# A fused attention, expert and gated-MLP kernel: its first pair of heads loaded, measured and transposed in another order

## The chip, the cores and the metric

The kernel runs on one NeuronCore of a Trainium2 chip. Its engines are TensorE (PE: matmuls and transposes, with PEld its weight loads), VectorE (DVE), ScalarE (ACT), GpSimd (POOL) and the sequencer SyncE (SP), and 16 DMA engines move data. Each engine works through its own instructions in the order in which they were written, and semaphores tie the engines together. The metric is the device time of one execution in microseconds, as the median of several runs.

## The reference

Three layers follow each other for 8 batches of 576 rows. The first is block-causal attention over 8 heads of 64, the second a mixture of four causal attention experts of which the best two are added, the third a gated MLP with a spatial mix over the rows.

```python
def _attn_ref(q, k, v):                       # 8 x 8 x 576 x 64
    scores = scale * np.matmul(q, k.transpose(0, 1, 3, 2))
    mask = block_i >= block_j                 # blocks of 64
    scores = np.where(mask, scores, -1000000000.0)
    scores = scores - np.max(scores, axis=-1, keepdims=True)
    attn = np.exp(scores)
    attn = attn / (np.sum(attn, axis=-1, keepdims=True) + 1e-09)
    return np.matmul(attn, v).astype(np.float32)

def _moe_ref(x, w_gate, wq, wk, wv, wo):      # 4 experts, 2 of them used
    logits = x @ w_gate
    for e in range(E):
        q = x @ wq[e]; k = x @ wk[e]; v = x @ wv[e]
        scores = np.where(causal, -1000000000.0, scale * (q @ k.transpose(0, 2, 1)))
        a = np.exp(scores - scores.max(-1, keepdims=True))
        a /= a.sum(-1, keepdims=True) + 1e-09
        out += (gate weight of e) * (a @ v @ wo[e])

def _moe2_ref(x, w_in, w_spatial, b_spatial, w_out):
    h = np.maximum(x @ w_in, 0.0)
    u, v = (h[..., :d_ff // 2], h[..., d_ff // 2:])
    v_n = (v - mu) / np.sqrt(var + 1e-06)
    v_s = np.einsum('ts,bsd->btd', w_spatial, v_n) + b_spatial[None, :, None]
    return ((u * v_s) @ w_out).astype(np.float32)
```

## The kernel before

Every float32 operand is scaled by a power of two and split into two float16 halves, a high and a low one, and each product is three float16 matmuls (high by high, high by low, low by high; `PROD`). The scale of an operand comes from its own size, so nothing can be split before its size is known. The work goes by batch, and in a batch by pairs of heads: four pairs of the attention, two pairs of the experts, and then the gated MLP.

A pair begins with loads. `load_qk` issues seven DMAs (line 257: both heads of q and both of k, 128 KB each; line 261: the last 64 rows of q, head by head; line 263: the last 64 rows of k) into a tile `nat`, and `load_v` three more (lines 271 and 274). `mags` then takes the size of the operand in each partition, on VectorE as a largest magnitude (line 297, written to `mst`) or on ScalarE as a sum of magnitudes (line 295, with its accumulator). In batches 1 to 7 one scale serves all four pairs. In batch 0 each pair has a scale of its own for q and k, so that the first pair doesn't wait for the others: `scale0` turns the two columns of sizes by a transpose on TensorE (line 200), takes their maxima (203), spreads them on a diagonal (206), and `scale2` sends that to all partitions by a matmul with ones (211) and makes powers of two of it on VectorE (218 to 227: `ne`, `sc`, `in`; 324 and 326: `es`). `prep_qk` transposes q and k on TensorE (line 345) and splits them: ScalarE writes the high half (233), VectorE the low one (239), both into `qk`. Then come the scores in four parts j = 0 to 3 (393, with a mask 403; 408 for j = 3), their row maxima on VectorE (414, 416), a bias (424 on ScalarE or 426 on VectorE), the exponentials on ScalarE (430, 435), the split of the weights (352 to 356, 451, 455), DMA transposes (460), the product with v (470), and the split of its result (499, 504), which another DMA transpose (506) brings into `x` for the dense part.

The constants and zeroed paddings at the kernel's head are memsets and selects on VectorE and GpSimd (lines 97 to 192, with line 371 further down); the memset in line 284 is the last of VectorE's before the first `mags`. The weights are loaded and split once, between the first pairs (`startup`). At the end of each batch the gated MLP normalises `vf` in five chunks of rows: line 921 shifts and scales, 924 casts on ScalarE, 929 subtracts, each chunk on VectorE or GpSimd as a letter in a table says.

The order is written out by hand in two tables. Some 1,370 steps (`add` lists them, with what each needs) are cut at every `yield` into pieces, `ORDER` names the step of each next piece, 3,671 entries in all, and `WAYS` names the engine for steps that could run on more than one ("D" VectorE, "A" ScalarE, "G" GpSimd, "S" SyncE for loads). In `WAYS`, the entry `lq.0` holds the queue of the first pair's `load_qk` for each batch, `mg.0.0` the engine of its first `mags`. The costs that `add` carries (`pe`, `act`, `dve`, `loads`) are the numbers with which the tables were planned; they don't enter the program. Loads on the SP and ACT queues take their semaphores in turn out of eight, so that the ninth load waits for the first to land.

In batch 0 a step `pq` (that is, `prep_qk`) needs the step `s2o` (`scale2` of the pair) before its first piece, the transposes, since its scale is used in the second.

Of the kernel before, what the change touches and what calls it, by code (L numbers as in the profile page):

```python
# [10 lines left out]
F32 = mybir.dt.float32  # L11
# [12 lines left out]
P = 128  # L24
# [12 lines left out]
def attn_moe_gmlp_kernel(  # L37
# [211 lines left out]
    def load_qk(b, pr, way):  # L249
        dma = dict(S=nc.sync, A=A, G=G)[way].dma_start  # L250
# [26 lines left out]
    def mags(b, pr, i, way):  # L277
# [8 lines left out]
        a = slice(0, 2) if i == 0 else slice(2, 3)  # L286
        st = s.st
        o = slice(pr, pr + 1)
        if b == 0 and i == 0:
            s.own[pr] = Obj()  # L290
            s.own[pr].st = st = cst.tile([P, 2, 1], F32, name=f"mst{pr}")
            o = slice(0, 1)
# [40 lines left out]
    def prep_qk(b, pr, i):  # L333

        p, s = PD[b, pr], BS[b]
        if b == 0:
            s = s.own[pr]
        if i == 0:
            new_qk(p)
            p.es, p.nes = s.es[:, 0:1], s.es[:, 1:2]  # L340
        ps = duo()
        n = 640 if i == 0 else 576
        for c in range(NC):
            r = P if c < 4 or i == 0 else 64
            T.transpose(ps[:, P * c:P * c + r], p.nat[0:r, i, c, :], ident[0:r, 0:r])
        yield
        o = (p.q, p.k)[i]
        yield from split16(o[:, 0], o[:, 1], ps[:, 0:n], s.sc[:, i:i + 1], "A")
# [416 lines left out]
    def dense(b, keep):  # L765
# [831 lines left out]
```

## Time and profile before

| | us |
|---|---|
| median of 3 runs | 933.75 |
| lowest and highest | 932.49 to 935.44 |
| the profiled execution | 931.44 |
| its span, from the first to the last instruction | 929.7 |
| PE busy | 838.6 (90%) |
| DVE busy | 754.4 (81%) |
| ACT busy | 632.9 (68%) |
| POOL busy | 547.5 (59%) |
| DMA engines, mean rate | 155 GB/s |

The rows come from one profiled execution, with times in microseconds from the start of its span. The shares of busy time are averages over stages that differ: the stretch before the first matmul, a stretch in which the first batches and the weights are prepared, a long one in which the batches follow each other, and the last batch's tail. "PEclk" is the clock that TensorE was granted as a share of its full 2.4 GHz; 0.50 is the lower level, 1.2 GHz.

### The profile page before, as it was taken

To read this page: it belongs to the slowest core of one execution; us is meant where nothing else is said; L and a number is where in the kernel's file an instruction comes from. 1 tells how busy PE (TensorE), PEld (TensorE's weight loads), DVE (VectorE), ACT (ScalarE), POOL (GpSimd) and SP (SyncE) were. 2 spreads that over 40 slices of the span, in tenths; PEclk is the share of its full clock that TensorE was granted. 3 is DMA by queue.
4 is the path that set the end of the run, shared out by engine and by line. 5 is a ranking of instruction groups with operands and counts; after the bars stand their busy time and mean duration, and the time that the engine had idled before them with its cause. 6 is when DMAs were issued, how large, how long until landed. Compare 5 with 4: busy or idle time off the path is not lost. (4 is left out here: it accounts for less than half of the span.)

```text
span 929.7 us, 25206 instructions
## 1 busy us (share of the span) xinstructions
PE 838.6 (90%) x10038; PEld 616.4 (66%) x10038; DVE 754.4 (81%) x1608; ACT 632.9 (68%) x1151; POOL 547.5 (59%) x542
## 2 busy tenths in 40 slices
PE   3677887789998999989999999989999999999987
PEld 2466765567766767666776677567767786667554
DVE  6999989988998688887988799788997879468351
ACT  3867687866778777785776697675698568448232
POOL 6557457756677767785675867345857665425120
PEclk9777999599999999999999999999999999999999
DMA  9999889998789798999799799879699939914601
GB/s 202 217 220 191 185 178 177 193 158 133 164 152 201 112 186 149 197 189 169 137 159 197 133 149 199 145 138 181 139 180 171 158 58 155 202 30 77 140 1 57
DMA packets 470716, 143.66 MB, mean 155 GB/s; under 512 B 456003, under 2 KB 462499, under 8 KB 470598
## 3 DMA queue, kind: packets, MB, share of 16 engines
q1 hardware_dynamic: 461750, 129.72, 78.4%
q0 software_dynamic: 5232, 11.44, 4.9%
q8 instruction: 79, 1.29, 0.5%
q10 hardware_dynamic: 3616, 0.89, 0.5%
q14 instruction: 39, 0.32, 0.1%
HBM read 38.19 MB, written 9.44 MB: 51 GB/s over the span
## 5 line engine op out<-in xcount | busy, mean ns | idle before, releaser
L455 POOL TENSOR_TENSOR p<-pf,p 128x512 f16<-128x512 f32 (+1 forms) x198 | 242.5, 1247 | 74.7 <-DVE p L354 24.8
L414 DVE TENSOR_REDUCE st<-duo 128x2 f32<-128x1024 f32 (+2 forms) x192 | 151.2, 814 | 17.5 <-PE duo L401 8.8
L470 PEld LDWEIGHTS <-pT 128*128 128x128 f16 x4320 | 144.6, 99 | 28.2 <-DMA pT<-p 12.9
L435 ACT ACTIVATE pf<-duo,st,es 128x512 f32<-128x512 f32 (+3 forms) x224 | 122.4, 617 | 17.0 <-DVE st L426 14.2
L393 PE MATMUL duo<-qk 64*128 64x256 f16 (+3 forms) x1152 | 110.9, 315 | 20.6 <-DVE qk L239 7.7
L356 POOL TENSOR_SCALAR p<-pf 128x1024 f16<-128x1024 f32 (+1 forms) x68 | 78.0, 1149 | 86.5 <-ACT pf L435 55.9
L980 PE MATMUL duo<-wsp,vn 128*128 128x288 f16 x832 | 111.9, 286 | 2.1 <-ACT pf L435 1.1
L470 PE MATMUL duo<-v,pT 128*128 128x65 f16 (+1 forms) x2880 | 102.3, 196 | 10.2 <-DMA pT<-p 5.4
L804 PE MATMUL duo<-x,wqk 128*128 128x288 f16 x768 | 98.7, 286 | 2.1 <-DVE pf L499 0.7
L980 PEld LDWEIGHTS <-vn 128*128 128x128 f16 x832 | 80.0, 98 | 24.0 <-DVE vn L929 1.6
L804 PEld LDWEIGHTS <-wqk 128*128 128x128 f16 x768 | 74.3, 98 | 21.9 <-issue 2.9
L998 PE MATMUL duo<-wo,gT 128*128 128x512 f16 x384 | 86.0, 379 | 0.2 <-POOL gT L987 0.2
L393 PEld LDWEIGHTS <-qk 64*128 64x128 f16 x1152 | 46.2, 98 | 52.5 <-issue 33.0
L921 POOL TENSOR_SCALAR vf<-vf,nw 128x512 f32<-128x512 f32 (+1 forms) x27 | 25.8, 963 | 82.7 <-DVE nw L912 36.6
L435 ACT ACTIVATE pf<-duo,st,mt 128x256 f32<-128x256 f32 (+3 forms) x128 | 69.8, 617 | 5.3 <-DVE st L426 4.0
L451 DVE TENSOR_TENSOR p<-pf,p 128x1024 f16<-128x1024 f32 (+1 forms) x45 | 64.6, 1436 | 6.1 <-ACT p L352 5.8
L998 PEld LDWEIGHTS <-gT 128*128 128x128 f16 x384 | 36.6, 98 | 43.3 <-DVE gT L987 1.0
L504 POOL TENSOR_TENSOR xh<-pf,xh 128x640 f16<-128x640 f32 x30 | 44.8, 1494 | 32.9 <-ACT xh L352 26.6
L827 PE MATMUL duo<-wvg,x 128*128 128x260 f16 x480 | 56.5, 274 | 0.6 <-DVE nw L912 0.6
L352 ACT CAST p<-pf 128x1024 f16<-128x1024 f32 (+1 forms) x53 | 56.7, 1072 | 0.5
L470 PE MATMUL duo<-V,pT 128*128 128x65 f16 (+1 forms) x1440 | 49.6, 194 | 7.8 <-DMA pT<-p 5.2
L883 PE MATMUL duo<-wf,x 128*128 128x512 f16 x240 | 54.5, 379 | 1.8 <-DMA x<-xh 1.2
(273 smaller groups left out, 1732.2 us busy)
## 6 DMA issues: line engine op xcount, KB each, us to landing
out_dram<-pf SPq DMA_DIRECT2D x16, 512.0 KB, 3.3
nat<-in_q_dram SPq DMA_DIRECT2D x40, 128.0 KB, 3.2
nat<-in_k_dram SPq DMA_DIRECT2D x40, 128.0 KB, 3.2
wf<-in_moe_w_in_dram SPq DMA_DIRECT2D x8, 512.0 KB, 5.3
nat<-in_v_dram SPq DMA_DIRECT2D x32, 128.0 KB, 3.0
nat<-in_v_dram POOLq DMA_DIRECT2D x30, 128.0 KB, 4.6
nat<-in_q_dram POOLq DMA_DIRECT2D x22, 128.0 KB, 4.4
nat<-in_k_dram POOLq DMA_DIRECT2D x22, 128.0 KB, 4.4
```

The lines of the kernel that those rows point to most:

```text
L352: A.copy(hi, src)
L356: G.tensor_scalar(hi, src, 1.0, 1.0, op0=OP.mult, op1=OP.mult)
L393: T.matmul(ph[:, hh, o:o + w], p.q[hs, a, ts], p.k[hs, bb, 0:w], start=i == 0, stop=False)
L414: V.reduce_max(st[:, 0, 2 * c:2 * c + 2], ph[:, :, off[c]:off[c] + P * (c + 1)], axis=AX.X)
L435: A.activation(pf[:, n * hh + off[c]:n * hh + off[c] + w], ph[:, hh, off[c]:off[c] + w], AF.Exp, bias=st[:, 1, 2 * c + hh:2 * c + hh + 1], ...
L451: V.tensor_sub(lo, src, hi)
L455: G.tensor_sub(lo[:, z:z + m], src[:, z:z + m], hi[:, z:z + m])
L470: T.matmul(ps[:, hh, o:o + n], pT[:, col(t, kk):col(t, kk) + P], p.v[:, hh, kk, a:a + n], start=kk == 0 and i == 0, stop=kk == nk - 1 and ...
L804: T.matmul(ps[:, MID + a:MID + a + w], wqk16[:, l, c, 2 * n + i, :], x16[c][:, r, a:a + w], start=m == 0, stop=m == 11)
L827: T.matmul(ps[:, i, :260], x16[d][:, l, P * c:P * c + P], wvg16[:, r, d, :], start=m == 0, stop=m == 11)
L980: T.matmul(ps[:, MID + a:MID + a + n], l, wsp16[:, r, c, a:a + n], start=i == 0, stop=i == 13)
L998: T.matmul(ps[:, i], gT[:, x, d, P * c:P * c + P], wo16[:, y, d, :], start=m == 0, stop=m == 11)
```

## The change

The seven loads of the first pair of batch 0 are issued ahead of all others and go in turn to the SP and the ACT queue (way "M"). Its sizes are taken by two engines: `mags` has three steps for this pair, q on VectorE, k on ScalarE, and v (as before) later. In batch 0 the transposes of `prep_qk` need only the loads, and the scale only from the second piece on. `ORDER` and `WAYS` are written anew for the whole kernel; most entries stand within a few places of where they stood, and 50 steps, most of them in batches 1 to 7, run on another engine than before.

```diff
     def load_qk(b, pr, way):
-        dma = dict(S=nc.sync, A=A, G=G)[way].dma_start
+        each = iter((nc.sync, A) * 4) if way == "M" else None
+
+        def dma(*a):
+            (next(each) if each else dict(S=nc.sync, A=A, G=G)[way]).dma_start(*a)
...
         a = slice(0, 2) if i == 0 else slice(2, 3)
+        if b == 0 and pr == 0:
+            a = (slice(0, 1), slice(2, 3), slice(1, 2))[i]
         st = s.st
         o = slice(pr, pr + 1)
-        if b == 0 and i == 0:
-            s.own[pr] = Obj()
-            s.own[pr].st = st = cst.tile([P, 2, 1], F32, name=f"mst{pr}")
+        if b == 0 and i != 1:
+            if pr not in s.own:
+                s.own[pr] = Obj()
+                s.own[pr].st = cst.tile([P, 2, 1], F32, name=f"mst{pr}")
+            st = s.own[pr].st
             o = slice(0, 1)
...
         if i == 0:
             new_qk(p)
-            p.es, p.nes = s.es[:, 0:1], s.es[:, 1:2]
         ps = duo()
...
         yield
+        p.es, p.nes = s.es[:, 0:1], s.es[:, 1:2]
         o = (p.q, p.k)[i]
...
-        50, 54, 54, 50, 51, 50, 50, 50, 54, 50, 50, 52, 142, 142, 142, 143, 143, 51, 54, 54, 143, 143, 143, 143, 54,
+        50, 50, 50, 50, 50, 50, 50, 55, 55, 51, 55, 54, 52, 67, 143, 68, 143, 143, 144, 144, 51, 55, 144, 144, 144,
...
-        "last": ("A", "G", "G", "G", "G", "G", "A", "D"), "lq.0": ("A", "S", "S", "S", "G", "S", "S", "G"),
+        "last": ("D", "G", "G", "G", "G", "G", "A", "D"), "lq.0": ("M", "S", "S", "S", "S", "S", "S", "G"),
...
-            for i in range(2):
+            one = key == (0, 0)
+            for i in range(2 + one):
...
-                    [("PE", 0.73), act(n, each=0.15), dve(n, rate=1.06)], [("s2", b) if b else ("s2o", key)], [("pq", key, 0)] * i,
-                    ["duo"] + [("qk", key)] * (i == 0), ["duo"])
+                    [("PE", 0.73), act(n, each=0.15), dve(n, rate=1.06)], [("s2", b) if b else ("lq", key)], [("pq", key, 0)] * i,
+                    ["duo"] + [("qk", key)] * (i == 0), ["duo"], {} if b else {1: [("s2o", key)]})
```

Lines from 250 on move: what was line 345 is 351 after the change, 297 is 304, and from 346 on every line stands 7 lower.

On TensorE, at the program's head, the rows before are these (`nat` is the loaded pair, `mst` the sizes, `dgo` the diagonal with the maxima, `qk` the split operands):

```order
L1592 UNCONDITIONAL_BRANCH
L200 MATMUL duo<-ident,mst_198 2x128
L211 MATMUL duo<-dgo,ones 128x2
L345 MATMUL duo<-ident,nat 128x128 x9
L345 MATMUL duo<-ident,nat 128x64
L200 MATMUL duo<-ident,mst_234 2x128
L393 LDWEIGHTS qk
```

And these after the change:

```order
L1603 UNCONDITIONAL_BRANCH
L351 MATMUL duo<-ident,nat 128x128 x5
L200 MATMUL duo<-ident,mst_198 2x128
L351 MATMUL duo<-ident,nat 128x128 x4
L351 MATMUL duo<-ident,nat 128x64
L211 MATMUL duo<-dgo,ones 128x2
L200 MATMUL duo<-ident,mst_236 2x128
```

The ten transposes of the first pair stood behind the two small matmuls of its scale; now the five of q stand ahead of both, and the five of k between them.

On ScalarE's queue, at the program's head, before (L257, L261 and L263 are `load_qk`, L271 and L274 `load_v`):

```order
L175 ACTIVATE junk<-ones 128x1
L257 DMA nat<-in_q_dram 128x4x64 x2
L271 DMA nat<-in_v_dram 128x4x64
L257 DMA nat<-in_k_dram 128x4x64 x2
L261 DMA nat<-in_q_dram 64x64 x2
L263 DMA nat<-in_k_dram 64x2x64
L271 DMA nat<-in_v_dram 128x4x64
L274 DMA nat<-in_v_dram 64x2x64
L233 ACTIVATE qk<-duo,sco_206 128x640
L233 ACTIVATE qk<-duo,sco_206 128x576
```

After (L253 is now every load of `load_qk`, L302 the sizes on ScalarE):

```order
L175 ACTIVATE junk<-ones 128x1
L253 DMA nat<-in_q_dram 128x4x64
L253 DMA nat<-in_k_dram 128x4x64
L253 DMA nat<-in_q_dram 64x64
L274 DMA nat<-in_v_dram 128x4x64
L302 ACTIVATE junk,mst_198<-nat 128x640
L274 DMA nat<-in_v_dram 128x4x64
L277 DMA nat<-in_v_dram 64x2x64
L233 ACTIVATE qk<-duo,sco_217 128x640
```

Three of the pair's seven loads stay on this queue instead of all seven, the first load of v goes behind them, and the sizes of k stand between two loads of v. The other four go to SyncE's queue, ahead of the second pair's loads, which had stood first there.

On VectorE in the last batch's normalisation, the rows between the last small operation on `nw` and the scale of h (`neh`) were these before:

```order
L912 TENSOR_SCALAR nw<-mv 128x5
L921 TENSOR_SCALAR vf<-vf,nw 128x512 x2
L921 TENSOR_SCALAR vf<-vf,nw 64x512
L929 TENSOR_TENSOR vn<-vf,vn 128x512 x3
L929 TENSOR_TENSOR vn<-vf,vn 64x512
```

And these after:

```order
L919 TENSOR_SCALAR nw<-mv 128x5
L928 TENSOR_SCALAR vf<-vf,nw 128x512 x3
L936 TENSOR_TENSOR vn<-vf,vn 128x512
L928 TENSOR_SCALAR vf<-vf,nw 64x512
L936 TENSOR_TENSOR vn<-vf,vn 128x512 x2
L936 TENSOR_TENSOR vn<-vf,vn 64x512
```

One more chunk is shifted on VectorE, and GpSimd has one instead of two.

## Rows read from the trace of the kernel before

**Rows 1.** Busy time by stage (stretch, length, then each engine's busy time with instructions).
```profile
0.00:20.00 20.00, 7.11 (x39) 4.06 (x39) 11.78 (x54) 5.12 (x9) 16.25 (x41) 1.00 0.96 201
20.00:180.00 160.00, 121.66 (x1374) 95.60 (x1374) 152.38 (x309) 124.28 (x231) 96.69 (x97) 0.82 1.00 196
180.00:200.00 20.00, 16.25 (x267) 13.03 (x267) 15.53 (x35) 12.04 (x22) 9.42 (x9) 0.83 1.00 167
200.00:800.00 600.00, 575.64 (x7285) 425.01 (x7285) 509.73 (x1045) 440.57 (x805) 393.12 (x368) 1.00 0.89 159
800.00:930.00 130.00, 117.97 (x1076) 78.67 (x1074) 64.94 (x169) 50.90 (x85) 32.00 (x29) 0.98 0.38 75
```

**Rows 2.** Timeline of the first 20 us: start, length, engine, line, operation, idle before.
```profile
2.67 1.09 ACTq L257 DMA_DIRECT2D nat<-in_k_dram  x2
...
6.58 0.66 ACTq L263 DMA_DIRECT2D nat<-in_k_dram  x1
...
7.66 0.07 DVE L284 MEMSET mst<- 128x8 f32 x1
...
8.18 0.65 SPq L263 DMA_DIRECT2D nat<-in_k_dram  x1
...
9.39 1.49 DVE L297 TENSOR_REDUCE mst<-nat 128x2 f32<-128x1280 f32 x1 [1.66 <-DMA nat<-in_k_dram]
...
11.02 0.37 PE L200 MATMUL duo<-ident,mst 128*2 128x128 f32 x1 [11.02 <-DVE mst L297]
...
12.38 0.56 PE L211 MATMUL duo<-dgo,ones 2*128 2x2 f32 x2 [0.99 <-DVE dgo L206]
...
12.87 2.48 PE L345 MATMUL duo<-ident,nat 128*128 128x128 f32 x10
12.98 0.16 DVE L218 TENSOR_SCALAR neo<-duo 128x2 int32<-128x2 int32 x1 [0.74 <-PE duo L211]
...
13.42 0.31 DVE L226 TENSOR_SCALAR sco<-neo 128x2 int32<-128x2 int32 x1
...
13.99 0.15 DVE L326 TENSOR_SCALAR eso<-eso 128x1 f32<-128x1 f32 x1
...
14.24 0.79 ACT L233 ACTIVATE qk<-duo,sco 128x640 f16<-128x640 f32 x1 [11.94 <-PE duo L345]
...
16.18 0.61 PE L393 MATMUL duo<-qk 64*128 64x512 f16 x2
...
17.03 0.61 PE L393 MATMUL duo<-qk 64*128 64x512 f16 x2 [0.24 <-DVE qk L239]
...
19.94 2.42 DVE L414 TENSOR_REDUCE st<-duo 128x2 f32<-128x768 f32 x3 [1.13 <-PE duo L403]
```

**Rows 3.** Two single microseconds: last come granted clock, DMA share and GB/s.
```profile
2.00:3.00 1.00, 0.00 (x0) 0.00 (x0) 0.89 (x5) 0.28 (x2) 0.62 (x2) 1.00 1.12 254
...
7.00:8.00 1.00, 0.00 (x0) 0.00 (x0) 0.72 (x16) 0.00 (x0) 0.99 (x2) 1.00 0.34 58
```

**Rows 4.** Groups of one shape over the whole run: busy us, mean ns, idle before.
```profile
L297 DVE TENSOR_REDUCE mst<-nat 128x1 f32<-128x640 f32 x13 | 10.5, 807 | 0.0
...
L295 ACT ACTIVATE junk<-nat 128x640 bf16<-128x640 f32 x57 | 42.0, 737 | 1.6 <-DMA nat<-in_k_dram 0.6
```

**Rows 5.** Stretches of 5 us with columns as in Rows 1, where TensorE's clock is halved.
```profile
155.00:160.00 5.00, 1.08 (x21) 0.70 (x21) 4.96 (x7) 4.94 (x11) 4.13 (x5) 0.94 1.01 193
...
180.00:185.00 5.00, 4.15 (x31) 2.74 (x31) 3.08 (x12) 3.25 (x6) 3.56 (x3) 0.50 1.08 205
185.00:190.00 5.00, 5.00 (x105) 4.69 (x104) 3.77 (x10) 3.90 (x8) 1.12 (x2) 0.83 0.50 95
```

**Rows 6.** Timeline of the last batch's normalisation.
```profile
890.28 1.75 DVE L921 TENSOR_SCALAR vf<-vf,nw 128x512 f32<-128x512 f32 x3
890.42 2.84 POOL L921 TENSOR_SCALAR vf<-vf,nw 128x512 f32<-128x512 f32 x2 [20.37 <-DVE nw L912]
...
893.95 2.31 DVE L929 TENSOR_TENSOR vn<-vf,vn 128x512 f16<-128x512 f32 x3 [1.33 <-ACT vn L924]
```

More of the change, by code (lines that the diff above doesn't have):

```diff
@@ L1396, in s1_steps @@
             due = t0 + S_DUE[pr]
-            add(("lq", key), due - 60, lambda w, key=key: load_qk(*key, w), loads([512] * 4 + [64] * 2 + [128]), acq=[("nat", key)], way="S")
+            ld = loads([512] * 4 + [64] * 2 + [128])
+            if key == (0, 0):
+                ld["M"] = [ld["SA"[n % 2]][n] for n in range(7)]
+            add(("lq", key), due - 60, lambda w, key=key: load_qk(*key, w), ld, acq=[("nat", key)], way="S")
             add(("lv", key), due - 59, lambda w, key=key: load_v(*key, w), loads([512] * 2 + [128]), after=[("lq", key)], way="S")
-            for i in range(2):
+            one = key == (0, 0)
+            for i in range(2 + one):
                 mg.append(("mg", key, i))
+                n = 640 if one or i else 1280
                 add(mg[-1], due - 50 + i, lambda w, key=key, i=i: mags(*key, i, w),
-                    dict(D=[dve((1280, 640)[i])], A=[act((1280, 640)[i], 2 - i, 0.27)]), [(("lq", "lv")[i], key)],
+                    dict(D=[dve(n)], A=[act(n, n // 640, 0.27)]), [(("lq", "lv", "lq")[i], key)],
                     way="D")
@@ L1419, in s1_steps @@
             key = (b, pr)
-            add(("s1o", key), t0 - 55 + 5 * pr, lambda pr=pr: scale0(b, pr), [("PE", 0.2), dve(128), tiny()], [("mg", key, 0)], [], ["duo"], ["duo:1"])
+            add(("s1o", key), t0 - 55 + 5 * pr, lambda pr=pr: scale0(b, pr), [("PE", 0.2), dve(128), tiny()], [("mg", key, 0)] + [("mg", key, 2)] * (pr == 0), [], ["duo"], ["duo:1"])
             add(("s2o", key), t0 - 54 + 5 * pr, lambda pr=pr: scale2(BS[b].own[pr], 2, f"o{pr}"),
```

401 rows, old and new, of tables (ORDER, WAYS) are left out of this document.

## The prediction

> **What bounds the kernel now.** I read busy time by stage first, since the averages over the span hide that four stages have four limits [rows 1]. Up to 20 us nothing is full: TensorE works 7.1 us and VectorE 11.8 us of 20. From 20 to 180 us VectorE is the bound, 152.4 of 160 us. From 200 to 800 us TensorE is, 575.6 of 600 us, and what it waits for there adds up to 24.4 us. In the tail one batch is left, and short chains decide again. Work that is moved off an engine pays only in the stage where that engine is full; a chain that gets shorter at the start pays if the stage behind it, which is full, can begin earlier and finds its data there.
>
> Then I followed the chain of the start in the timeline [rows 2]. VectorE ends its memsets at 7.66 + 0.07 = 7.73 and stands until 9.39, since the last piece of the first pair's k is issued on ACT's queue only at 6.58. The sizes of q and k take it to 10.88. Small operations lead from there over the transposes of the sizes (11.02) and the matmul with ones (12.38) to the scale, which is done at 13.42 + 0.31 = 13.73. Only then ScalarE could split q, but it starts at 14.24, after the transposes that began at 12.87. The scores begin at 16.18, their second product at 17.03, and the first row maxima on VectorE at 19.94. That last row is the point at which VectorE's full stage begins.
>
> **The change, part by part.** *Loads.* In the row of ACT's queue three loads of the pair come before anything that waits, and SP has the other four. Two DMAs took 1.01 to 1.09 us to issue there, some 0.5 us each [rows 2], so that SP, which starts within the first microsecond, has issued its fourth by about 2.9. The pair's q and k are 4 x 128 + 2 x 16 + 32 = 576 KB; the engines moved 254 KB per us as soon as they moved anything, at 2 us [rows 3]. That makes an estimate of 2.0 + 2.3 = 4.3 us if nothing else moved, and of 5.7 us with the last piece's own way to landing, for which I take what k's last piece had on ACT's queue: issued at 6.58, and VectorE started at 9.39, so at most 2.8 us, here behind 2.9. Both ends lie before 7.73. So VectorE's own memsets are what is late next, and the 1.66 us of waiting go whole.
>
> *Sizes.* VectorE's reduce falls from 1.49 us to the 0.81 us of one operand [rows 2, 4]: it ends at 7.73 + 0.81 = 8.54 instead of 10.88. ScalarE's share (0.74 us [rows 4] and the reading of its sum) starts when k has landed, at about 5.7, and is covered unless k lands after 7.6. Behind it on ACT's queue stand only two loads of v, which no row of these 20 us reads.
>
> *Transposes.* From the end of the reduce to the matmul with ones it was 12.38 - 10.88 = 1.50 us. Now five transposes of k stand in between, at 2.48 / 10 = 0.25 us each [rows 2]: the small transpose starts at 8.68, lasts 0.37, and they end at 9.05 + 1.25 = 10.30, against 8.54 + 1.50 = 10.04. They cost 0.26 us there, and take 2.48 us away from behind the scale. With the matmul at 10.30 the scale is done 13.73 - 12.38 = 1.35 us later, at 11.65. ScalarE has q's high half at about 12.55 and k's at 13.35, and the scores begin at 13.4 instead of 16.18, a gain of 2.8.
>
> *What comes behind.* The second product needs k's low half from VectorE. VectorE finishes the first pair's small operations at 10.30 + (14.14 - 12.38) = 12.06, takes the second pair's sizes (1.49), then q's low half and k's, 0.8 each, to 15.2. The second product thus starts at about 15.3 instead of 17.03, a gain of 1.7, and since q's low half, which came second before, is there too, the third product has no wait of its own. The first row maxima gain between 1.7 and 2.8; I take the middle, **2.3 us**.
>
> *Does it last?* From 20 to 180 us VectorE's work is what it was; its one shorter instruction lies in the chain above. So the stage begins 2.3 us earlier and, if its data are there, ends 2.3 us earlier.
>
> *The new tables.* Between 200 and 800 us the same matmuls run on the bound. A new order can give back at most the 24.4 us that TensorE stands, or add to them; most entries moved only a few places, and I take 0, with 2 us to either side. In the tail a chunk of the normalisation goes from GpSimd to VectorE. GpSimd took 2.84 us for two, VectorE 1.75 for three, 0.58 each, and three subtractions followed from 893.95 to 896.26 [rows 6]. Now VectorE shifts three chunks by 892.03, subtracts once (0.77), shifts the short one by 893.4 and ends its last three subtractions at 895.7 at the latest: **0.6 us** earlier, and TensorE's last matmuls over the rows wait for just that.
>
> *Sum.* 2.3 + 0.6 = 2.9 us off the profiled execution's 931.44, or 928.5. That execution lies 2.3 below the median of 933.75; the same offset gives **930.8**.
>
> **A rule of the Trainium skill.** What the rows show is 254 KB per us in the third microsecond, with both queues issuing [rows 3]. "DMA: Bandwidth & Descriptors", section "Issuing engines are not separate DMA queues", says that loads started from several engines run on the same 16 DMA engines and interleave, so that a second queue saves only the time of issuing. The trace agrees as far as the rate is full at once. By that rule the pair's earlier landing is paid by whoever is issued behind it.
>
> **The rivals.** *Swallowed by the second pair.* Its seven loads stood first on SP and now stand behind four, partly waiting for semaphores of earlier ones; its last piece was issued at 8.18 before [rows 2]. VectorE wants it at 12.06 now, 2.1 us earlier than before (right behind the row that ends at 14.14). For it: the engines' rate is full in these microseconds, and they are bytes that don't get fewer. Against it: at 7 to 8 us the DMA engines were busy a third of the time [rows 3], so there is room. If it lands at 14.2, the sizes, the low halves and the maxima are where they were; only the tail's 0.6 is left, 930.8 by the profile and 933.1 by the median.
>
> *The lower clock lasts longer, and the kernel is slower.* At 155 to 160 us TensorE works 1.08 of 5 us, its clock falls, and it runs at 0.50 (1.2 GHz) for most of the time to 185 [rows 5]. While VectorE is full that costs nothing; from 180 on VectorE has 3.08 of 5 and TensorE is the one waited for. Each microsecond at the lower clock is half lost there. Should the new order leave such a gap later, so that twelve more microseconds run at half the clock, 6.0 - 2.9 = 3.1 us are lost: 934.5 by the profile, 936.8 by the median. It decides the sign from six microseconds on. For it: the order of 160 us is written anew. Against it: VectorE's work, which makes the gap, isn't more.
>
> *The lower clock ends sooner.* The same from the other side: if TensorE has its full clock at 180, its 4.15 us to 185 and about 1.7 us at half clock behind them take half as long [rows 5], 2.9 us more: 927.9 by the median.
>
> *It doesn't do what it says.* If k's sum on ScalarE comes after 8.5, the small transpose waits for it. k would have to land 1.9 us later than I have it; the price is what it is later than that, within the range.
>
> **How the numbers follow.** A measurement of this kernel can tell about 0.3% from no change, 2.8 us, so the border to faster is 930.95, just above my forecast. The forecast, with 929 to 932.5 around it, has 0.50, of which I put 0.30 below the border. The sooner end of the lower clock has 0.17, all faster. Swallowed has 0.20, all within 0.3%. Slower has 0.13. That makes faster 0.47, same 0.40, slower 0.13. The range goes from 926.8 (the clock's gain with one more microsecond from the tables) to 935.0 (swallowed, with 2 us lost by the tables); a tenth lies on either side.
>
> **What would show it.** The first reduce starts at 7.7 and lasts 0.8; the transposes of q are done before it ends; the scale is done near 11.65, the scores begin near 13.4, the first row maxima on VectorE near 17.6. VectorE's row for 20 to 180 us holds the same busy time, and the dense part of batch 0 begins as much earlier. If VectorE stands before the second pair's sizes, the rival has it. If the start gains 2.3 us and the end doesn't, the clock's rows from 155 to 190 us or the 24.4 us of the long stage must have changed. The forecast is wrong if VectorE isn't what the first 180 us hang on.

## The result: 1.3% slower, and the profile after

The changed kernel takes 946.53 us (median of 4 runs, 944.98 to 948.12) where the kernel before, run beside it, takes 934.60. The ratio is 1.013, with a 95% interval of 1.0103 to 1.0157. The profiled execution took 944.98 us, 13.5 more than the one of before. Both are single executions, and the kernel before took from 929.85 to 945.09 us over all its runs, so that a few us between two traces need not come from the change. 930.8 was predicted, and 926.8 to 935.0 as the range.

Busy time by stage, in the columns of [rows 1]:

```profile
0.00:20.00 20.00, 8.81 (x50) 5.17 (x50) 13.89 (x60) 7.04 (x14) 16.24 (x41) 1.00 0.97 210
20.00:180.00 160.00, 117.64 (x1363) 92.87 (x1364) 149.43 (x302) 123.04 (x230) 96.37 (x96) 0.82 1.03 195
180.00:200.00 20.00, 14.82 (x267) 11.62 (x267) 16.24 (x35) 11.53 (x21) 10.39 (x9) 0.88 0.91 151
200.00:800.00 600.00, 568.86 (x7080) 418.35 (x7080) 494.27 (x1024) 427.41 (x785) 389.58 (x363) 0.99 0.85 155
800.00:930.00 130.00, 123.83 (x1243) 85.31 (x1244) 74.74 (x187) 61.64 (x105) 37.71 (x34) 0.97 0.48 86
```

In the first 20 us more is done than before. The loss is in the fourth row: TensorE works 568.86 us of 600 instead of 575.64, and its clock is 0.99 instead of 1.00.

The start did what it was meant to. The timeline of the first 20 us (start, length, engine, line, operation; compare [rows 2]):

```profile
5.84 0.74 ACT L302 ACTIVATE junk<-nat 128x640 bf16<-128x640 f32 x1 [3.55 <-DMA nat<-in_k_dram]
...
7.65 0.80 DVE L304 TENSOR_REDUCE mst<-nat 128x1 f32<-128x640 f32 x1
...
8.77 1.38 PE L351 MATMUL duo<-ident,nat 128*128 128x128 f32 x5
...
11.95 1.49 DVE L304 TENSOR_REDUCE mst<-nat 128x2 f32<-128x1280 f32 x1
...
13.49 0.37 PE L200 MATMUL duo<-ident,mst 128*2 128x128 f32 x1 [2.83 <-DVE mst L304]
13.79 0.61 PE L400 MATMUL duo<-qk 64*128 64x512 f16 x2
15.00 1.03 PE L400 MATMUL duo<-qk 64*128 64x512 f16 x4 [0.60 <-DVE qk L239]
...
16.13 1.23 DVE L421 TENSOR_REDUCE st<-duo 128x2 f32<-128x1024 f32 x1
...
17.52 1.29 DVE L421 TENSOR_REDUCE st<-duo 128x2 f32<-128x768 f32 x2 [0.17 <-PE duo L410]
```

The first reduce starts right behind VectorE's memsets, the scores begin at 13.79 (13.4 forecast, 16.18 before), and the first row maxima at 16.13, 3.8 us earlier than before; 2.3 had been taken. The two first maxima are not the same work, though. The kernel before takes those of 768 columns first, at 19.94 [rows 2], and those of 1,024 columns, whose scores come first, only at 21.15; the new order takes the 1,024 first. The maxima of 768 columns go from 19.94 to 17.52, which is 2.4 us. The rest of the 3.8 is the new order of the maxima and not a shorter chain.

To see where the time goes I took, for each batch, the moment at which the first small operation of its dense part starts on VectorE (`begin`, L778 before, L785 after). The second row is the kernel before, the others the difference from it, in us:

| batch | 0 | 1 | 2 | 3 | 4 | 5 | 6 | 7 |
|---|---|---|---|---|---|---|---|---|
| before, at | 119.5 | 204.2 | 310.1 | 416.7 | 510.2 | 615.3 | 704.8 | 813.2 |
| after | -0.8 | +0.1 | +2.9 | +3.4 | +7.8 | +13.4 | +13.7 | +13.9 |

So 0.8 us of the start's gain is left at 119 us, and none at 204. Nearly all the loss comes between 204 and 629 us, in three steps (2.8, 4.4 and 5.6 us); 0.5 us is added behind. In those stretches TensorE stands (it waits and does nothing), and in this trace its clock is halved behind each of these stands:

```profile
265.00:270.00 5.00, 2.96 (x22) 1.77 (x20) 5.00 (x5) 0.74 (x1) 4.29 (x5) 1.00 0.74 150
270.00:275.00 5.00, 4.78 (x90) 3.60 (x91) 4.88 (x7) 2.78 (x5) 1.75 (x2) 0.66 0.63 148
410.00:415.00 5.00, 2.89 (x74) 2.77 (x71) 3.87 (x4) 4.15 (x9) 4.91 (x4) 0.84 1.21 179
415.00:420.00 5.00, 5.00 (x58) 3.87 (x56) 3.95 (x7) 2.92 (x6) 3.40 (x3) 0.82 1.13 150
435.00:440.00 5.00, 2.31 (x35) 1.54 (x35) 4.91 (x10) 2.95 (x4) 0.47 (x1) 1.00 1.00 209
440.00:445.00 5.00, 4.14 (x21) 2.75 (x21) 2.98 (x20) 0.00 (x0) 1.53 (x3) 0.66 0.51 107
540.00:545.00 5.00, 3.19 (x33) 1.55 (x32) 4.93 (x8) 1.99 (x3) 4.32 (x5) 1.00 0.85 179
545.00:550.00 5.00, 4.20 (x12) 1.56 (x12) 4.97 (x11) 1.83 (x3) 4.47 (x4) 0.66 0.01 3
620.00:625.00 5.00, 3.65 (x50) 2.75 (x47) 4.88 (x9) 4.23 (x9) 4.45 (x4) 1.00 0.80 108
625.00:630.00 5.00, 5.00 (x76) 3.80 (x75) 4.68 (x12) 2.78 (x6) 0.36 (x1) 0.66 0.71 111
```

Between 200 and 800 us the kernel before has no stretch of 5 us below the full clock; [rows 1] has 1.00 there. Two sums make up the loss: TensorE stands 600 - 568.86 = 31.1 us instead of 24.4, 6.8 more; and in the halved stretches it loses, by an estimate, its busy time times what is missing at the clock, 4.78 x 0.34 + 2.89 x 0.16 + 5.00 x 0.18 + 4.14 x 0.34 + 4.20 x 0.34 + 5.00 x 0.34 = 7.5 us. Together they are 14.3; by the table it is 13.9 - 0.1 = 13.8 from batch 1 to batch 7. With 0.3 less in the tail (from `begin` of batch 7 to the end 116.2 instead of 116.5) this is the 13.5 us by which the profiled executions differ.

What TensorE waits for is told by the waits between 200 and 830 us (engine, tile and line, what released it; us in total, times, longest):

```profile
PE duo L811 <- DVE neh L218: 3.6, 1, 3.6
PE duo L890 <- DVE cmh L203: 2.6, 1, 2.6
```

In the kernel before these two are 0.3 and 0.6 us. They make up most of the 6.8 us by which TensorE stands longer. The longest of them, at 437 us, begins on VectorE. After:

```profile
436.31 2.42 DVE L421 TENSOR_REDUCE st<-duo 128x2 f32<-128x1024 f32 x3
...
438.64 1.28 DVE L898 BATCH_NORM_STATS2 bs<-vf 128x6 f32<-128x512 f32 x2
...
440.66 0.15 DVE L218 TENSOR_SCALAR neh<-duo 128x1 int32<-128x1 int32 x1
...
440.86 4.68 PE L811 MATMUL duo<-x,wqk 128*128 128x288 f16 x24 [3.56 <-DVE neh L218]
```

And the same place before, at 432 us:

```profile
432.34 1.23 DVE L414 TENSOR_REDUCE st<-duo 128x2 f32<-128x1024 f32 x1 [0.97 <-PE duo L403]
...
433.49 0.15 DVE L218 TENSOR_SCALAR neh<-duo 128x1 int32<-128x1 int32 x1
...
433.69 3.10 PE L804 MATMUL duo<-x,wqk 128*128 128x288 f16 x24 [0.34 <-DVE neh L218]
```

L218 reads the scale of batch 2's gated part from a PSUM tile that the projection of the next batch (L811, L804 before) needs. It is 0.15 us long and stood behind one score maximum; in the new order it stands behind three, two statistics, two aggregates and three small steps, which keep VectorE from 436.31 to 440.66. TensorE waits 3.56 us for it, and then runs the 24 matmuls in 4.68 us instead of 3.10.

### The profile page after: what moved, and what is told of

The parts are those of the page before. It is cut to its first block, busy times and chain, and to the rows that moved or that the text cites. A ratio compares the mean times of both kernels' runs of the same rounds, so it can differ in the third digit from the quotient of the medians.

```text
span 943.3 us, 25207 instructions
## 1 busy us (share of the span) xinstructions
PE 842.3 (89%) x10038; PEld 616.9 (65%) x10038; DVE 748.6 (79%) x1602; ACT 634.2 (67%) x1155; POOL 550.3 (58%) x541
## 4 chain that ended last, share of the span: by engine, by line
PE 44%; DVE 10%; DMA 5%; ACT 4%; issue 2%; POOL 2%; DVEq 0%; ACTq 0%; POOLq 0%
PE duo L987 7%; PE duo L811 6%; PE duo L1005 6%; PE duo L477 6%; DMA pT<-p 5%; PE duo L890 4%; PE duo L834 3%; PE duo L971 3%; PE duo L400 3%; DVE st L421 3%; ACT pf L442 2%; POOL p L462 1%; PE duo L415 1%; PE duo L351 1%; DVE p L458 1%
## 5 line engine op out<-in xcount | busy, mean ns | idle before, releaser
L462 POOL TENSOR_TENSOR p<-pf,p 128x512 f16<-128x512 f32 (+1 forms) x202 | 245.8, 1240 | 73.4 <-DVE p L361 32.3
L400 PE MATMUL duo<-qk 64*128 64x256 f16 (+3 forms) x1152 | 112.8, 320 | 23.2 <-DVE qk L239 12.0
L363 POOL TENSOR_SCALAR p<-pf 128x1024 f16<-128x1024 f32 (+1 forms) x68 | 80.5, 1185 | 85.9 <-ACT pf L442 49.8
L811 PE MATMUL duo<-x,wqk 128*128 128x288 f16 x768 | 100.4, 289 | 5.5 <-DVE neh L218 3.8
L811 PEld LDWEIGHTS <-wqk 128*128 128x128 f16 x768 | 74.8, 99 | 26.1 <-issue 6.3
L928 POOL TENSOR_SCALAR vf<-vf,nw 128x512 f32<-128x512 f32 (+1 forms) x26 | 22.1, 858 | 90.7 <-DVE nw L919 74.0
L458 DVE TENSOR_TENSOR p<-pf,p 128x1024 f16<-128x1024 f32 (+1 forms) x43 | 55.1, 1282 | 5.8 <-ACT p L359 4.7
L351 PE MATMUL duo<-ident,nat 128*128 128x128 f32 (+1 forms) x320 | 51.0, 290 | 8.9 <-DMA nat<-in_q_dram 4.6
L890 PE MATMUL duo<-wf,x 128*128 128x512 f16 x240 | 56.1, 387 | 3.2 <-DVE cmh L203 2.6
L233 ACT ACTIVATE qk<-duo,scb 128x640 f16<-128x640 f32 (+1 forms) x56 | 42.0, 767 | 22.8 <-PE duo L351 21.3
```

What stands on the lines that cost most here:

```text
L363: G.tensor_scalar(hi, src, 1.0, 1.0, op0=OP.mult, op1=OP.mult)
L400: T.matmul(ph[:, hh, o:o + w], p.q[hs, a, ts], p.k[hs, bb, 0:w], start=i == 0, stop=False)
L458: V.tensor_sub(lo, src, hi)
L462: G.tensor_sub(lo[:, z:z + m], src[:, z:z + m], hi[:, z:z + m])
L811: T.matmul(ps[:, MID + a:MID + a + w], wqk16[:, l, c, 2 * n + i, :], x16[c][:, r, a:a + w], start=m == 0, stop=m == 11)
L890: T.matmul(ps[:, i], h16[d][:, l, P * c:P * c + P], wf16[:, r, d, FH:], start=m == 0, stop=m == 5)
```

## The experiments

Theory 1: the start gains what was predicted, and the two rewritten tables lose some 15 us. Rival: an earlier start itself shifts the engines against each other. Ratios are to the kernel before, run beside each.

**1. The changed start on the old tables.**

The changed kernel's code and the first 53 entries of its `ORDER`; all other entries and `WAYS` are those of the kernel before, but for

```diff
-        "lq.0": ("A", "S", "S", "S", "G", "S", "S", "G"),
+        "lq.0": ("M", "S", "S", "S", "G", "S", "S", "G"),
+        "mg.0.2": ("A",),
```

> The changed kernel's code at the start (loads first and from two queues, the maxima split over two engines, transposes ahead of the scale), the first 53 pieces in the changed order, and from there on the order and the engine choices of the kernel before. Theory 1 (the start gains 1 to 3 us, and the rewritten tables lose some 15 us in the stage that TensorE bounds): 930 to 934 us, no stretch at the lower clock between 200 and 815 us, TensorE idle there for about the 24.4 us of [rows 1]. Rival (an earlier start itself shifts the engines against each other later, whatever the tables): 940 us or more, with the halved stretches of the changed kernel.

933.97 us, ratio 0.9963 (0.9926 to 1.0001). The stage from 200 to 800 us:

```profile
200.00:800.00 600.00, 574.87 (x7248) 424.10 (x7246) 507.85 (x1045) 439.21 (x804) 392.27 (x367) 1.00 0.88 157
```

TensorE stands 25.1 us and has its full clock from 205 us on. The rival is out: the same early start (first row maxima at 16.13 here too) with the old tables loses nothing.

**2. The old start on the new tables.** The code of before and its first 41 entries, then order and choices of the changed kernel; against that kernel's `WAYS`

```diff
-        "lq.0": ("M", "S", "S", "S", "S", "S", "S", "G"),
+        "lq.0": ("A", "S", "S", "S", "S", "S", "S", "G"),
-        "mg.0.2": ("A",),
```

> The code of the kernel before (first pair's loads from one queue, maxima by VectorE alone, transposes behind the scale) and its order for the first 41 pieces, then the order and the engine choices of the changed kernel. Theory 1 (the tables lose): 946 to 950 us, with several stretches at the lower clock between 225 and 815 us. Rival (the earlier start is what disturbs the later stages): about 934 us and no such stretch.

945.99 us, ratio 1.0116 (1.0063 to 1.017); halved stretches at 270 and 440 us, two where several were expected. The tables lose without the start's change. Its `begin` differs from the kernel before by +0.3, +1.4, +4.0, +3.8, +7.8, +11.7, +12.1, +12.3 us: the steps of the changed kernel, in the same batches. TensorE stands 32.9 us from 200 to 800 us, 8.5 more than before, and the halved clock costs 2.7 by the same estimate.

**3 and 4. Order and engine choices apart.** The changed kernel with the engine choices of before (3), and the kernel of experiment 1 with the new choices (4). Two of the 49 steps whose engine differs, as in 4 against 1:

```diff
-        "last": ("A", "G", "G", "G", "G", "G", "A", "D"),
+        "last": ("D", "G", "G", "G", "G", "G", "A", "D"),
-        "lq.0": ("M", "S", "S", "S", "G", "S", "S", "G"),
+        "lq.0": ("M", "S", "S", "S", "S", "S", "S", "G"),
```

> The changed kernel with its own order but the engine choices of the kernel before (except the two that the split maxima and the two queues need). If the order carries the loss: 943 to 949 us. If the engine choices carry it: 930 to 935 us. If the loss needs order and choices of one plan together, this one is as slow or slower too, 943 to 955 us, and so is its counterpart with the old order and the new choices.

> The changed kernel with the order of the kernel before behind the first 53 pieces, but all its own engine choices. If the order carries the loss: 930 to 935 us. If the engine choices carry it: 943 to 949 us. If any mismatch of order and choices costs: 940 to 955 us.

The new order with the old choices takes 965.68 us (1.032, 1.0279 to 1.0361), the old order with the new choices 941.74 (1.0057, 1.003 to 1.0083). The first is slower than any range that had been given for it. Both mixtures are slower than the kernel of experiment 1, and the new order suits its own choices better than the old ones. So the loss can't be divided between order and choices. My reading is that both tables are one plan, in which an entry's place is right only for the lengths it was planned with; beyond these two times it isn't shown.

**5. One stand mended.** On VectorE, against the changed kernel:

```diff
-L421 TENSOR_REDUCE st<-duo 128x2 x3
+L421 TENSOR_REDUCE st<-duo 128x2
+L218 TENSOR_SCALAR neh<-duo 128x1
+L421 TENSOR_REDUCE st<-duo 128x2 x2
...
-L218 TENSOR_SCALAR neh<-duo 128x1
```

> The changed kernel with one entry of its order moved up by eight places: the scale step of batch 2 on VectorE (L218, 0.15 us) stands again ahead of two score maxima, three statistics and three small steps. Theory 2 (each stand of TensorE of some 2.5 us or more between 225 and 815 us costs itself and the stretch at the lower clock behind it, and neither is given back): the wait of 3.56 us for neh at 437.3 and the halved stretch behind it (0.66 over 440 to 445) go, the product at L811 starts then, and the kernel gets 3.4 + 1.7 = 5 us shorter, 941 to 942 us. Rival (TensorE's stand there only hides other waits that come up next): 945 to 947 us, with a stand of a like size within 20 us of it.

The entry moves up by seven places, not eight. 940.61 us, ratio 1.0035 (1.0012 to 1.0058), against 1.013 of the changed kernel: about 6 us by the medians, up to 9 by the ratios, where 5 were expected. The columns are again those of [rows 1]:

```profile
435.00:440.00 5.00, 5.00 (x45) 2.58 (x45) 4.54 (x10) 2.15 (x3) 2.25 (x3) 1.00 0.83 168
440.00:445.00 5.00, 4.66 (x78) 3.94 (x75) 4.76 (x20) 3.00 (x6) 0.00 (x0) 1.00 1.01 220
```

From `begin` of batch 3 to that of batch 4 it takes 93.6 us (before 93.5, after 97.8). What was lost there is back, and no wait came in its place.

The same trace limits the theory. The stand at L890, which this kernel doesn't mend, is there as before, and behind it TensorE keeps its full clock:

```profile
544.16 2.75 PE L890 MATMUL duo<-wf,x 128*128 128x512 f16 x12 [2.64 <-DVE cmh L203]
```

```profile
545.00:550.00 5.00, 5.00 (x54) 3.54 (x53) 4.97 (x14) 4.19 (x8) 2.92 (x3) 1.00 0.29 66
```

In experiment 2 it is the same: the stand at L890 is 2.61 us, and the clock stays at 1.00 from 540 to 550 us. So a stand of this size costs the clock behind it in some executions and not in others.

**6. The same stand put into the kernel before.** L218 moved down by seven entries; on VectorE:

```diff
-L218 TENSOR_SCALAR neh<-duo 128x1
...
 L898 TENSOR_SCALAR nw<-mv 128x5
 L414 TENSOR_REDUCE st<-duo 128x2 x2
 L900 TENSOR_SCALAR nw<-nw 128x5
 L902 TENSOR_SCALAR nw<-nw 128x5
+L218 TENSOR_SCALAR neh<-duo 128x1
```

> The kernel before, with the scale step of batch 2 moved down by seven entries, to where the changed kernel has it. Theory 2: TensorE stands some 3.5 us at 433.7, its clock is halved behind that for about 3.4 us, and the kernel gets 5 us longer: 939 to 941 us beside 934 to 936. Rival (given back later): within 2 us of the kernel before.

941.14 us, ratio 1.005 (1.0028 to 1.0072), which is 4.7 us (5 expected). The stand and the clock behind it:

```profile
442.60 0.15 DVE L218 TENSOR_SCALAR neh<-duo 128x1 int32<-128x1 int32 x1
...
442.80 5.88 PE L804 MATMUL duo<-x,wqk 128*128 128x288 f16 x24 [4.21 <-DVE neh L218]
```

```profile
440.00:445.00 5.00, 2.20 (x10) 1.37 (x10) 4.80 (x25) 0.76 (x2) 0.00 (x0) 0.67 0.97 210
445.00:450.00 5.00, 5.00 (x65) 3.60 (x64) 0.87 (x4) 1.26 (x4) 2.54 (x3) 0.65 0.02 5
```

One entry of 3,671, moved by seven places, costs the kernel before half a per cent (0.3 to 0.7). Experiments 5 and 6 show this stand from both sides.

**7. Three stands mended.** The stands near 268 and 544 us also hang on VectorE, but there by an instruction that takes many times its usual length. After:

```profile
261.72 0.75 POOL L253 DMA_DIRECT2D nat<-in_q_dram  x1 [0.65 <-PE duo L351]
...
261.89 4.98 DVE L994 TENSOR_TENSOR gT<-u,gT 128x576 f16<-128x576 f32 x1
262.49 2.28 POOL L462 TENSOR_TENSOR p<-pf,p 128x512 f16<-128x512 f32 x2
264.73 1.04 POOL L363 TENSOR_SCALAR p<-pf 128x1024 f16<-128x1024 f32 x1
```

```profile
540.93 0.80 POOL L253 DMA_DIRECT2D nat<-in_k_dram  x1
...
541.10 3.09 DVE L851 TENSOR_TENSOR win<-lg 128x5 f32<-128x5 f32 x1
...
541.76 2.39 POOL L462 TENSOR_TENSOR p<-pf,p 128x544 f16<-128x544 f32 x2
...
545.47 0.27 DVE L203 TENSOR_REDUCE cmh<-duo 1x1 f32<-1x128 f32 x1
...
545.80 0.38 PE L890 MATMUL duo<-wf,x 128*128 128x512 f16 x1 [2.60 <-DVE cmh L203]
```

The subtraction L994 usually takes 0.75 us and L851 0.16. On VectorE's queue the maximum L203, for which TensorE waits, stands behind the second of them.

L218 is moved up as in 5, and besides, on VectorE in batch 0 and in batch 4 (L850 to L858 are the gate):

```diff
+L994 TENSOR_TENSOR gT<-u,gT 128x576
 L239 SCALAR_TENSOR_TENSOR v<-nat,scb,v 128x10x64
 L989 TENSOR_TENSOR u<-duo,u 128x576
 L433 TENSOR_SCALAR st<-st,mt 128x2
-L994 TENSOR_TENSOR gT<-u,gT 128x576
...
+L239 SCALAR_TENSOR_TENSOR v<-nat,scb,v 128x10x64
+L203 TENSOR_REDUCE cmh<-duo 1x1
 L850 TENSOR_TENSOR win<-lg 128x5x3
...
 L858 TENSOR_TENSOR g<-lg,gs 128x20
-L239 SCALAR_TENSOR_TENSOR v<-nat,scb,v 128x10x64
-L203 TENSOR_REDUCE cmh<-duo 1x1
```

> The changed kernel with four entries moved: the scale step of batch 2 as above; batch 4's first two gate steps on VectorE put behind the column maximum that TensorE waits for at 543 us (one of their instructions takes 3.09 us there instead of 0.16); batch 0's subtraction gT at L994, which takes 4.98 us at 261.9, put ahead of the wait before it. Theory 2: 5 us for the first, 2.6 + 1.7 = 4.3 for the second, 2 + 1.7 = 3.7 for the third, so 946.5 - 13 = 933.5 us, 931 to 938; no halved stretch at 270, 440 and 545, those at 412 and 627 stay. Rival (other waits come up): above 940 us.

939.07 us, ratio 1.002 (0.9997 to 1.0043). That is a miss: 933.5 had been expected. The first mend holds. The second takes the wait at L890 away, but a wait of 1.85 us for ScalarE comes up at L811 behind it, as the rival says: from `begin` of batch 4 to that of batch 5 it takes 109.4 us, and in experiment 5, without this mend, 109.3 (before 105.1). The third does nothing: L994 now takes 1.06 us, and the long instruction is the next one on VectorE, which usually takes 0.22:

```profile
262.61 0.76 POOL L253 DMA_DIRECT2D nat<-in_q_dram  x1 [0.64 <-PE duo L351]
...
263.20 3.49 DVE L433 TENSOR_SCALAR st<-st,mt 128x2 f32<-128x2 f32 x1
...
263.38 2.28 POOL L462 TENSOR_TENSOR p<-pf,p 128x512 f16<-128x512 f32 x2
...
265.62 1.05 POOL L363 TENSOR_SCALAR p<-pf 128x1024 f16<-128x1024 f32 x1
```

It ends at 266.69, when GpSimd ends its block (265.62 + 1.05 = 266.67). So the length goes not with the instruction but with its place beside GpSimd's work.

**8. GpSimd's work moved instead.** Against the kernel of 7, on GpSimd (L994 on VectorE stands where the changed kernel has it):

```diff
-L462 TENSOR_TENSOR p_142<-pf,p_142 128x512 x2
 L363 TENSOR_SCALAR p_142<-pf 128x1024
 L253 DMA nat<-in_q_dram 128x4x64
 L363 TENSOR_SCALAR p_142<-pf 128x1088
+L462 TENSOR_TENSOR p_142<-pf,p_142 128x512 x2
```

> The changed kernel with the scale step of batch 2 moved up and the gate steps of batch 4 moved down as in the three-fold mend, but instead of the subtraction on VectorE it is GpSimd's double subtraction of 2.28 us (L462, two halves of 128x512) that is moved, behind GpSimd's next copies, as in the kernel before. If what holds VectorE at 262 to 266 us is that GpSimd runs that subtraction there: gT at L994 takes 0.75 us instead of 4.98, L433 0.2 instead of 3.49 (its length in the three-fold mend), TensorE's stand and the halved stretch near 270 go, begin of batch 2 comes 3 us earlier than in the three-fold mend, and the kernel takes 935 to 936 us. If VectorE's long instruction has another cause: as long as the three-fold mend, 938 to 940 us, with some instruction of VectorE over 3 us in that place.

934.26 us, ratio 0.9995 (0.9976 to 1.0014): within the bound of no change from the kernel before, and 1.3% off the changed kernel, by four moved entries. The intervals of experiments 7 and 8 overlap, so what GpSimd's entry alone is worth is read from the traces: from `begin` of batch 1 to that of batch 2 it takes 105.5 us (before 105.9, after 108.7, experiment 7 109.0), with no halved clock near 270. One number missed: L994 takes 2.93 us, not 0.75, since GpSimd still issues a load as it begins and copies for 1.06 us behind that:

```profile
264.29 0.75 POOL L253 DMA_DIRECT2D nat<-in_q_dram  x1 [0.65 <-PE duo L351]
...
264.46 2.93 DVE L994 TENSOR_TENSOR gT<-u,gT 128x576 f16<-128x576 f32 x1
...
265.06 1.06 POOL L363 TENSOR_SCALAR p<-pf 128x1024 f16<-128x1024 f32 x1
```

GpSimd's block behind the load is 3.28 us long in the changed kernel (262.49 to 265.77) and 1.06 here, 2.22 less, and VectorE's instruction gets 2.05 shorter.

**9 to 11. The parts of the start**, each undone alone in the kernel of experiment 1: all seven loads on one queue ("lq.0" back to "A"), both sizes on VectorE ("mg.0.2" to "D"), and the transposes behind the scale in the order. In 9 and 10, and on TensorE in 11:

```diff
-        "lq.0": ("M", "S", "S", "S", "G", "S", "S", "G"),
+        "lq.0": ("A", "S", "S", "S", "G", "S", "S", "G"),
...
-        "mg.0.2": ("A",),
+        "mg.0.2": ("D",),
...
-L351 MATMUL duo<-ident,nat 128x128 x5
 L200 MATMUL duo<-ident,mst_198 2x128
-L351 MATMUL duo<-ident,nat 128x128 x4
+L211 MATMUL duo<-dgo,ones 128x2
+L351 MATMUL duo<-ident,nat 128x128 x9
 L351 MATMUL duo<-ident,nat 128x64
-L211 MATMUL duo<-dgo,ones 128x2
```

Each ran once; what counts is when the first row maxima start. (The second of these expectations speaks of sums of squares; the sizes are largest magnitudes on VectorE and sums of magnitudes on ScalarE.)

> The kernel with the changed start and the old tables (of the first experiment), but the first pair's seven loads all from ScalarE's queue, as before, still ahead of the others. If the second queue matters: the first transposes of q still start near 4 us, but the last of k's loads are issued some 2 us later, and k's sum on ScalarE ends near 8.5 instead of 6.7 us; the first reduce on VectorE still starts at 7.7 (its own clears hold it), the first scores near 14.5 instead of 13.8. If it doesn't matter: scores within 0.2 us of 13.8.

> The kernel with the changed start and the old tables, but both of the first pair's sums of squares on VectorE, one behind the other (two reduces of 0.80 us instead of one beside ScalarE's). The column sums on TensorE then begin 0.8 us later, and with them scale, operands and scores: scores at 14.6 instead of 13.8 us.

> The kernel with the changed start and the old tables, but the first pair's transposes put behind the scale in the order, as before. TensorE then transposes only behind the two products of the scale (L211, end near 10.7 us), 1.5 us for q and as much for k; by the step of the prediction that moves them, the scaled operands come 0.5 to 1.5 us later and the scores begin at 14.3 to 15.3 instead of 13.8 us.

They start at 17.04, 16.89 and 15.87 us, against 16.13 with all parts. The second queue is worth 0.9 us and the second engine 0.8, near what was expected. Without the early transposes the first maxima start not later but 0.26 us *earlier*, where 0.5 to 1.5 us later had been expected for the scores: there the scale is ready sooner, with it VectorE's reduce of the second pair (L304, 1.49 us), and VectorE's low halves behind that reduce are what the second product waits for. That part of the change gives nothing. The times of these single runs (939.06, 931.91 and 936.66 us, and 941.71 for the kernel before beside the last two) vary by more than a microsecond of the start could tell.

**12. The earliest start of these, timed.** The kernel of 11, with transposes behind the scale.

> The kernel with the changed start, the old tables and the first pair's transposes behind the scale (the kernel of the last single look, whose first row maxima begin earliest of all, at 15.87 us), timed. If a start 4 us earlier is kept to the end: 931 to 932 us beside 935.5, a ratio of 0.996. If the stages behind swallow it: 934 to 936 us, a ratio of 0.999 to 1.001.

932.50 us beside 933.62, ratio 0.9978 (0.9958 to 0.9997). This lies between the two expectations. By the ratio 2.1 us of the start's 4.1 reach the end, but the interval goes from 0.3 to 3.9 us, and experiment 1, with 0.9963, is not distinguishable from it. It is clearly faster than the changed kernel; that it is faster than the kernel before is only just shown.

## Why the prediction was wrong

**Loads, sizes, chain of the start: right.** The loads land well before 7.73 (k's size starts at 5.84), VectorE's memsets were indeed next, the scale is done at 11.48 (11.65 forecast), and the rivals of a late second pair and of a late sum on ScalarE didn't come: the second pair's reduce starts at 11.95 without a wait. The maxima with which the kernel before began came 2.4 us earlier, 2.3 forecast. That others now begin at 16.13, 3.8 us earlier, lies in the order of the maxima, which the prediction didn't look at.

**The transposes: wrong in their reason.** Moved ahead or not, the scores begin at 13.8. In the changed kernel they stand on TensorE behind the second pair's small transpose (L200, 13.49), and that waits for VectorE's reduce, which ends at 13.44; the prediction had left this transpose out of the chain. In experiment 11 they begin at 13.77 and wait last for ScalarE's high half of k (0.17 us).

**Does it last: in the changed kernel hardly.** The prediction had VectorE as the bound up to 180 us, with the same busy time. Its row fell from 152.38 to 149.43 us. From the first row maxima to `begin` of batch 0 VectorE works as long as before (94.6 us), but it stands 8.0 us instead of 4.9, which takes back 3.1 of the 3.8 us. The longest of these waits is for ScalarE, in the preparation of the weights:

```profile
83.22 0.43 DVE L546 TENSOR_SCALAR x<-x 128x512 f32<-128x512 f32 x1 [2.45 <-ACT x L544]
```

ScalarE itself had stood 7.68 us until 78.75, since the size of a later k (L302), which comes ahead of L544 in its queue, waited for its load. In experiment 1, with the old tables, no size on ScalarE waits so long for a load, L544 runs at 80.56 instead of 82.54, and `begin` of batch 0 comes 2.1 us earlier than before. To the end, experiments 1 and 12 gain 0.37% and 0.22%, 3.5 and 2.1 us, where 2.3 had been taken. Their intervals (-0.1 to 6.9 and 0.3 to 3.9 us) allow 2.3 but don't show it.

**The tail: the chunk's work as forecast, its effect not shown.** 0.6 us were forecast for the moved chunk. The last batch's normalisation takes 5.56 us in all five kernels with the new order and the new choices, against 5.98 before, so 0.4 is gained there. But the stretch from `begin` of batch 7 to the end is 116.1 to 116.9 us in these five, and 115.8 to 116.5 in the seven with the old tables: nothing of it can be seen at the end.

**The new tables: this step failed.** "A new order can give back at most the 24.4 us that TensorE stands, or add to them; most entries moved only a few places, and I take 0, with 2 us to either side." It measured +14.3 us in the trace (6.8 of stands and 7.5 of clock), and experiment 2, which has the tables alone, is 10.9 us slower by its ratio. Two things in the step were wrong. The number of places says nothing of the cost: experiment 6 moves one entry by seven places and pays 4.7 us, because a 0.15 us instruction fell behind some 4 us of other work on its queue (from 438.81 to 442.60) with TensorE waiting for it. And a stand was not priced with the clock that can fall behind it, though [rows 5] showed such a fall. The slower rival had this mechanism, "should the new order leave such a gap later", but sought it at the one place where the trace already had a gap, and gave it 0.13. The 2 us to either side came from no row; a single moved entry cost more than that, so a rewritten order deserved a much wider term on the side of the loss. The prediction's own sign pointed to the place: it named the 24.4 us of the long stage as what must have changed if the start gains and the end doesn't.

**What stays open.** The stand near 412 us (2.11 us for a DMA transpose) and the one near 622 us were not mended on their own, so their share is read from the rows alone; experiment 8 still has the clock halved at 412. How much of the loss is clock isn't settled: it is 7.5 us in the changed kernel's trace and 2.7 in experiment 2's, whose `begin` is nearly as late. Halved stretches between 205 and 800 us are no mark of the new tables either: the traces of experiments 9, 10 and 12, with the old ones, have one each (at 381, 611 and 681 us). With the same first 20 us, batch 0's `begin` comes 2.1 us earlier than before in experiment 1 and 1.9 later in experiment 5; TensorE's clock between 20 and 200 us differs from trace to trace, and how much of the start's gain it takes isn't settled.

## To carry to other kernels

A hand-written order is part of the kernel's speed: change the start under the old tables, and look at every queue on which a short instruction, awaited by the bound engine, has come to stand behind long ones. Price a stand of TensorE with the clock that may fall behind it; here that was from nothing (L890 in experiments 2 and 5) to about as much again (the changed kernel's trace). When an instruction takes many times its usual length, look at what the other engine runs beside it before moving the instruction.

## What the runs showed of the hardware

Some of VectorE's instructions that begin while GpSimd issues a load last until GpSimd's computing behind that load has ended: L851 from 541.10 to 544.19 (GpSimd ends 544.15) at 3.09 us for 0.16, and L433 to 266.69 (GpSimd 266.67) at 3.49 for 0.22. L994, at 4.98 and 2.93 for 0.75, ends 1.1 and 1.3 us behind GpSimd's block and follows its length. Others that begin so are not held. In the changed kernel GpSimd issues a load from 539.11 to 539.86; an L850 and an L851 begin within it and take 0.18 and 0.17 us, and the next one is held:

```profile
539.63 1.41 DVE L850 TENSOR_TENSOR win<-lg 128x10 f32<-128x10 f32 x1
```

It ends at 541.04, when GpSimd's copy behind the load ends (541.00). What tells the held ones from the others isn't shown here. The Trainium skill says in "SBUF — State Buffer", section "SBUF: two separate sides", that VectorE and GpSimd share one pair of ports as an exclusive lock, which whoever starts first keeps for its whole instruction; for VectorE it names the instructions in a two-port mode, and those with two inputs in SBUF against a GpSimd instruction that reads SBUF. The ends in these rows agree with a lock, the order of the starts doesn't plainly: L851 began at 541.10, ahead of the instruction of GpSimd at 541.76 with which it ends. That the hold goes from a load's issue over one or two instructions behind it is what these rows add.
